# A routed-expert kernel on one Trainium2 core: gathers and row-number transfers held in program order, and another order of the composites

## The chip, the cores and the metric

The kernel runs on one core of one Trainium2 chip. The metric is the device time of one execution in microseconds (us). The core's engines are called as the profile calls them: PE is TensorE (PEld its weight loads), DVE VectorE, ACT ScalarE, POOL GpSimd, SP SyncE. SP only issues transfers here; POOL issues the indirect ones.

## What is computed

Two stages on an input `x` of 8 x 2880 x 192. First a causal 7-tap convolution per head, with softmax-normalised taps. Then each of the N = 23040 tokens is routed in two levels (the best of 4 groups, then the best of that group's 4 experts), and its one expert's two-layer network is applied:

```
x = attn_out.reshape(B * S, D)                    # 23040 x 192
g_idx = argmax(x @ w_group);  g_w = softmax(...)[g_idx]
for g in range(4):
    e_idx = argmax(x[g_idx == g] @ w_expert[g]);  e_w = softmax(...)[e_idx]
    for e in range(4):
        h  = maximum(xg[mask_e] @ w1[g, e], 0.0)  # 192 -> 1024
        ye = h @ w2[g, e]                         # 1024 -> 192
        out[tok_idx] = (g_w * e_w)[:, None] * ye
```

## The kernel before

**Units.** Convolution and routing run in units, mixed into the first half of the span. They write each token's row (196 numbers, its routing weight among them) to `xcd` in memory, and each token's row number into a table `idtab`, sorted by expert. When all tokens are routed, the table is closed: `close_table` writes 16 fills behind the experts' ends (L856, shown as `idtab<-seen`, on SP).

**Plan.** Expert work is a list of slots. The first 64 are full slots of 256 rows in three portions (one, two and one slot of each of the 16 experts); their row numbers are tiles `idp`. What each expert has left goes into 16 *composites*, whose row numbers are the tile `idpt`. A composite has one or two pieces, with row counts in `PIECES`: composites 0 and 1 are 320 + 320, 5 to 8 are 128 + 320, 9 to 11 are 384, 12 and 13 are 320, 14 and 15 are 256. `RANKS` is the order in which the composites run. Each full slot and each piece is a slot of the plan.

**One slot.** `gather` fetches its rows by indirect transfer on POOL (L674), 128 rows to a tile, into one of four buffers `xg`; a slot of 320 rows has a third tile of 64 rows, one of 384 a third of 128. The 64 full slots have no third tile. `turn` transposes the tiles on PE (L689, L690). `hidden` (L710; `hidden_wide`, L787, for over 256 rows) is the first layer, `back` (L728, L732; wide L805, L811) the second. `finish` scales on ACT (L822), adds the two halves on DVE (L829; a 64-row tile by L826 and L827), and stores through POOL (L830).

**Weights.** `weights` loads one expert's matrices on SP's queue by four transfers (L623, L624 and twice L626) into a ring of raw buffers; each is then split into a high and a low part by ACT and DVE (on DVE L639 for `al`, L643 for `bb`, L651 for `cw`).

**Opening the tail.** `open_tail` is a generator that is stepped at each opened slot: it closes the table, and then for each composite in the order of `RANKS` reads where its rows begin (L1046, SP) and transfers its row numbers (`tail_ids`, L1093 and, for a 64-row piece, L1095, `idpt<-idtab`, SP).

**Order.** A scheduler orders each engine's instructions; it may put an instruction ahead of others on its engine unless a dependence or an explicit hold binds it. Instructions then run in that order on each engine, each waiting for its own inputs and buffers.

**Rare block.** Tokens beyond the fixed plan are handled in a block under `tc.If` (L1190), which this input does not enter. It stands in front of the last slot of the plan; before it, all that is pending is finished.

Of the kernel before, what the change touches and what calls it, by code (L numbers as in the profile page):

```python
# [1 line left out]

# [12 lines left out]
U32 = mybir.dt.uint32  # L15
# [3 lines left out]
ET = mybir.EngineType  # L19
# [12 lines left out]
OOB_WHY = "the table's entries are clamped by construction"  # L32
# [3 lines left out]
def conv_moe_kernel(  # L36
# [10 lines left out]
    nc = tc.nc  # L47
# [9 lines left out]
    def pin(on, ins):  # L57

        return tc.keep_in_program_order(ins) if on and pinned[0] else ins
# [19 lines left out]
    PIECES = (  # L79
        [(320, 320)] * 2 + [(320, 256)] * 2 + [(256, 256)] + [(128, 320)] * 4 + [(384,)] * 3 + [(320,)] * 2 + [(256,)] * 2)  # L80
    CAPS = [sum(p) for p in PIECES]
    MOST, WMAX = CAPS[0], max(w for p in PIECES for w in p)
    NTAIL = len(PIECES)
    RANKS = [5, 2, 6, 3, 7, 4, 8, 0, 9, 14, 1, 10, 12, 11, 13, 15]
    assert NTAIL == E and sorted(RANKS) == list(range(E)) and sorted(CAPS, reverse=True) == CAPS
    CAP = -(-(N + MOST) // 1024) * 1024
    DUMMY = E * CAP
# [102 lines left out]
    xcd = dram.tile([N, XW], F32, name="xcd")  # L190
# [102 lines left out]
    for g in range(NSK):  # L293
        nc.sync.dma_start(
            out=skew[0:R, g * HG:(g + 1) * HG],
            in_=bass.AP(wvd.tensor, wvd.offset + VL - KS - (BT - 1) + g * HG * VL, [[1, R], [VL, HG], [1, VW]]),
# [15 lines left out]
    for h in range(H):  # L312
        nc.scalar.activation(
            out=band[0:R, h], in_=skew[0:R, h, BT - 1::-1], func=AF.Exp, bias=wm[0:R, h:h + 1],
# [10 lines left out]
    for k, (p0, r0, n) in enumerate(((0, 0, P), (0, P, D2), (D2, P, D2))):  # L325
# [10 lines left out]
        out=tri, in_=ones, pattern=[[1, P]], compare_op=ALU.is_gt, fill=0.0, base=0, channel_multiplier=-1,  # L336
# [10 lines left out]
    for nb in sorted({n for _, n in units}):  # L347
# [32 lines left out]
        out=sel[:, 0:E], in_=ident.rearrange("p (e l) -> p e l", e=E), axis=AX.X, op=ALU.add)  # L380
    nc.gpsimd.iota(io[:, 0:1], pattern=[[0, 1]], base=0, channel_multiplier=1)
    nc.vector.tensor_scalar(
        out=io[:, 1:2], in0=io[:, 0:1], scalar1=LE - 1, scalar2=None, op0=ALU.bitwise_and)
# [8 lines left out]
        out=eold[:, :, E:E + 1], in_=goff.unsqueeze(1).broadcast_to([P, NU + 1, 1]))  # L392
# [219 lines left out]
        finished(u)  # L612


    def weights(r1, r2, eng=None):
        eng = eng or {}
        raw = [wraw.tile([P, F], F32, name="raw") for _ in range(4)]
        ra, rb = raw[0], raw[1]
        HF = NF // 2
        rc = [r[:, 0:HF * D].rearrange("p (f d) -> p f d", d=D) for r in raw[2:]]  # L620
        npin[0] += 1
        hold = tc.keep_in_program_order if NPIN[0] < npin[0] <= NPIN[1] else lambda ins: ins
        hold(nc.sync.dma_start(out=ra, in_=w1f[bass.ds(r1, P), :]))  # L623
        hold(nc.sync.dma_start(out=rb[0:D2], in_=w1f[bass.ds(r1 + P, D2), :]))  # L624
        for k in range(2):
            hold(nc.sync.dma_start(  # L626
                out=rc[k], in_=w2f[bass.ds(r2 + k * HF * P, HF * P), :].rearrange("(f p) d -> p f d", p=P),
            ))
        W = {}

        def split(k):
            if k == 0:
                W["ah"] = ah = wsp.tile([P, F], F32R, name="ah")
                W["al"] = al = wsp.tile([P, F], F32R, name="al")
                if 8 in eng:
                    nc.gpsimd.tensor_copy(out=ah, in_=ra)
                else:
                    pin(PINA, nc.scalar.activation(out=ah, in_=ra, func=AF.Copy))  # L638
                eng.get(k, nc.vector).tensor_tensor(out=al, in0=ra, in1=ah.bitcast(F32), op=ALU.subtract)  # L639
            elif k == 1:  # L640
                W["bb"] = bb = wsp.tile([P, F], F32R, name="bb")
                pin(PINB, nc.scalar.activation(out=bb[0:D2], in_=rb[0:D2], func=AF.Copy))
                eng.get(k, nc.vector).tensor_tensor(  # L643
                    out=bb[D2:P], in0=rb[0:D2], in1=bb[0:D2].bitcast(F32), op=ALU.subtract)
            else:
                if k == 2:
                    W["cw"] = wsp.tile([P, NF, 2, D], F32R, name="cw")
                cw = W["cw"]
                fs = slice((k - 2) * HF, (k - 1) * HF)
                pin(PINW, nc.scalar.activation(out=cw[:, fs, 0, :], in_=rc[k - 2], func=AF.Copy))  # L650
                eng.get(k, nc.vector).tensor_tensor(  # L651
                    out=cw[:, fs, 1, :], in0=rc[k - 2], in1=cw[:, fs, 0, :].bitcast(F32), op=ALU.subtract,
                )

        W["todo"] = [lambda k=k: split(k) for k in range(4)]
        return W
# [9 lines left out]
    def split_rows(w):  # L666

        return [min(P, w - k) for k in range(0, w, P)]

    def gather(ids, known, w=SLOT):  # L670
        xs = xg[nslot[0] % NXG]
        nslot[0] += 1
        for t, n in enumerate(split_rows(w)):
            nc.gpsimd.indirect_dma_start(  # L674
                out=xs[0:n, t, :], out_offset=None, in_=xcd[0:known, :],
                in_offset=bass.IndirectOffsetOnAxis(ap=ids[t].bitcast(U32), axis=0),
                bounds_check=known - 1, oob_is_err=False,
            )
        return xs

    def turn(xs, w=SLOT):
# [156 lines left out]
    def close_table():  # L838
        ei = const.tile([1, E], I32, name="ei")
        nc.vector.tensor_copy(out=ei, in_=eold[0:1, counted[0], 0:E])  # L840
        yield

        NR = MOST // P
        seen = const.tile([P, NR], I32, name="seen")
        nc.sync.dma_start(
            out=seen, in_=TABV[0:NR, :].rearrange("r c -> (r c)").unsqueeze(0).broadcast_to([P, NR]))
        yield
        yield
        tc.keep_in_program_order(nc.vector.tensor_scalar(
            out=seen, in0=seen, scalar1=0, scalar2=BIG, op0=ALU.bitwise_and, op1=ALU.bitwise_or))  # L850
        yield
        _, ends = nc.values_load_multi_w_load_instructions(
            ei, engines=[ET.SP], min_val=0, max_val=DUMMY - MOST, skip_runtime_bounds_check_because=OOB_WHY,
        )
        for e in range(E):
            nc.sync.dma_start(  # L856
                out=idviews[1 + e % (len(idviews) - 1)][bass.ds(ends[e], MOST), :].rearrange("(p r) c -> p (r c)", p=P),
                in_=seen,
            )
            if e % 4 == 3:  # L860
                yield
# [171 lines left out]
    tab = [None]  # L1033
# [3 lines left out]
    idps = {}  # L1037
    late = []

    def open_tail():  # L1040
        yield from close_table()
        for tab[0] in table():
            yield
        idps["tail"] = const.tile([P, NTAIL, NID], I32, name="idpt")
        for j in RANKS:
            row = nc.values_load(  # L1046
                tab[0][0:1, j, 2:3], engines=[ET.SP], min_val=0, max_val=DUMMY,
                skip_runtime_bounds_check_because=OOB_WHY,
            )
            tail_ids(row, idps["tail"][:, j], PIECES[j])  # L1050
            yield

    def open_portion(pi):
# [35 lines left out]
    def tail_ids(row, idt, pieces=(SLOT,)):  # L1089
        n = sum(w // P for w in pieces)  # L1090
        m = sum(pieces) // XT - 2 * n
        rows = idtab[bass.ds(row, sum(pieces)), :]
        nc.sync.dma_start(out=idt[:, 0:n], in_=rows[0:n * P].rearrange("(p r) c -> p (r c)", r=n))  # L1093
        if m:
            nc.sync.dma_start(  # L1095
                out=idt[0:XT, n:n + m], in_=rows[n * P:n * P + m * XT].rearrange("(p r) c -> p (r c)", r=m))
# [8 lines left out]
    plan = [(pi, e, s) for pi, (_, spe) in enumerate(portions) for e in range(E) for s in range(spe)]  # L1105
    plan += [("tail", j, k) for j in RANKS for k in range(len(PIECES[j]))]
    weights_at = {}
# [44 lines left out]
    while routed[1] < portions[0][0]:  # L1152
        step()
        if k == 4:
            clear_table()
        for i in [i for i, kk in enumerate(KPRE) if kk == k]:
            e, q = divmod(i, 5)
            if q == 0 and e < 2:
                pre[e] = weights(e * D, e * F, {k: nc.gpsimd for k in PREG[e]})
            elif e < 2 and 4 * e + q <= KN:  # L1160
                split_one(pre[e])
        k += 1
# [83 lines left out]
    for i, (pi, e, s) in enumerate(plan):  # L1246
# [3 lines left out]
        W, ids = opened[i]  # L1250
        w = width(i)
        n = min(w, SLOT) // P
# [89 lines left out]
```

## Time and profile before

| | us |
|---|---|
| median of 3 runs | 1144.63 |
| lowest and highest | 1143.6, 1149.39 |
| the profiled execution | 1137.87 |
| span of the profiled execution | 1136.1 |
| mean granted clock of PE in it | 0.979 of full speed |

The profile is of one execution. A timeline row gives the start, the duration, the engine, the line and operation, out<-in, and, in brackets, how long the engine stood idle before it and what ended that. A q behind an engine's name (SPq, DVEq) is its sequencer, which issues transfers and runs branches. The granted clock of 1.00 is the higher of PE's two levels, 2.4 GHz, and 0.50 the lower, 1.2 GHz.

### The profile page before, as it was taken

To read this page: it belongs to the slowest core of one execution; us is meant where nothing else is said; L and a number is where in the kernel's file an instruction comes from. 1 tells how busy PE (TensorE), PEld (TensorE's weight loads), DVE (VectorE), ACT (ScalarE), POOL (GpSimd) and SP (SyncE) were. 2 spreads that over 40 slices of the span, in tenths; PEclk is the share of its full clock that TensorE was granted. 3 is DMA by queue.
4 is the path that set the end of the run, shared out by engine and by line. 5 is a ranking of instruction groups with operands and counts; after the bars stand their busy time and mean duration, and the time that the engine had idled before them with its cause. 6 is when DMAs were issued, how large, how long until landed. Compare 5 with 4: busy or idle time off the path is not lost. (4 is left out here: it accounts for less than half of the span.)

```text
span 1136.1 us, 23048 instructions
## 1 busy us (share of the span) xinstructions
PE 1087.7 (96%) x8170; PEld 1060.3 (93%) x8170; DVE 794.3 (70%) x1761; ACT 719.6 (63%) x1427; POOL 461.7 (41%) x420
## 2 busy tenths in 40 slices
PE   6799999999999999999999996999999999999995
PEld 5679899999999999999999996999999999999995
DVE  3747967887866666675678665888876766767772
ACT  4545576666775665656655664777776666666661
POOL 2003432234342534343435435555455454454531
PEclk9978999999999999999999998999999999999998
DMA  8879778879873564435354446777764444444420
GB/s 198 239 182 240 187 180 210 222 171 244 215 204 115 127 165 119 132 99 152 99 140 102 128 83 175 208 207 209 201 179 109 120 122 118 121 118 123 121 79 20
DMA packets 185203, 175.68 MB, mean 155 GB/s; under 512 B 47101, under 2 KB 166938, under 8 KB 185082
## 3 DMA queue, kind: packets, MB, share of 16 engines
q1 hardware_dynamic: 120108, 120.00, 39.2%
q0 software_dynamic: 18336, 36.08, 11.4%
q10 hardware_dynamic: 46638, 18.07, 7.4%
q8 instruction: 65, 1.06, 0.4%
q14 instruction: 56, 0.46, 0.1%
HBM read 138.23 MB, written 36.47 MB: 154 GB/s over the span
## 5 line engine op out<-in xcount | busy, mean ns | idle before, releaser
L728 PE MATMUL po<-cw,hh 128*128 128x384 f32 x1120 | 353.0, 372 | 0.4 <-ACT ys L822 0.4
L710 PE MATMUL ph<-xa,ah 128*128 128x256 f32 x1120 | 307.8, 296 | 4.4 <-DVEq L1190 2.4
L732 PE MATMUL po<-cw,hl 128*128 128x192 f32 x1120 | 281.2, 251 | 0.0
L715 ACT ACTIVATE hh<-ph 128x512 fp32r<-128x512 f32 x280 | 166.3, 595 | 162.7 <-PE ph L710 150.3
L674 POOL DMA_INDIRECT xg<-xcd,idp x128 | 143.1, 1118 | 306.6 <-ACT ys L822 275.6
L716 DVE SCALAR_TENSOR_TENSOR hl<-ph,hh 128x512 fp32r<-128x512 f32 x280 | 191.3, 686 | 92.9 <-ACT hh L715 89.7
L710 PE MATMUL ph<-xb,bb 128*128 128x256 f32 x1120 | 226.0, 283 | 0.0
L710 PEld LDWEIGHTS ph<-xa,ah 128*128 128x128 f32 x1120 | 212.3, 190 | 7.7 <-issue 2.7
L732 PEld LDWEIGHTS po<-cw,hl 128*128 128x128 f32 x1120 | 214.8, 192 | 1.9
L728 PEld LDWEIGHTS po<-cw,hh 128*128 128x128 f32 x1120 | 211.7, 189 | 2.9 <-ACT ys L822 0.6
L830 POOL DMA_INDIRECT out<-ys,idp x128 | 155.5, 1215 | 48.4 <-issue 30.1
L710 PEld LDWEIGHTS ph<-xb,bb 128*128 128x128 f32 x1120 | 173.2, 190 | 0.0
L710 PE MATMUL ph<-xa,al 128*128 128x256 f32 x560 | 158.3, 283 | 0.0
L822 ACT ACTIVATE ys<-po,xg 128x384 f32<-128x384 f32 x174 | 99.4, 581 | 77.2 <-PE po L732 41.5
L651 DVE TENSOR_TENSOR cw<-raw,cw 128x768 fp32r<-128x768 f32 x128 | 121.6, 952 | 19.3 <-ACT cw L650 17.4
L674 POOL DMA_INDIRECT xg<-xcd,idpt x61 | 69.2, 1135 | 136.7 <-ACT ys L822 95.2
L829 DVE TENSOR_TENSOR ys<-ys 128x192 f32<-128x192 f32 x177 | 62.6, 356 | 77.3 <-ACT ys L822 76.4
L650 ACT ACTIVATE cw<-raw 128x768 fp32r<-128x768 f32 x128 | 107.1, 842 | 4.2 <-DMA raw<-in_moe_w 4.1
L710 PEld LDWEIGHTS ph<-xa,al 128*128 128x128 f32 x560 | 107.5, 192 | 1.8
L639 DVE TENSOR_TENSOR al<-raw,ah 128x1024 fp32r<-128x1024 f32 x64 | 78.1, 1220 | 31.8 <-ACT ah L638 31.3
L830 POOL DMA_INDIRECT out<-ys,idpt x61 | 70.3, 1153 | 50.2 <-DVE ys L829 33.4
L638 ACT ACTIVATE ah<-raw 128x1024 fp32r<-128x1024 f32 x64 | 68.1, 1064 | 23.3 <-PE ph L710 10.1
(238 smaller groups left out, 1979.5 us busy)
## 6 DMA issues: line engine op xcount, KB each, us to landing
raw<-in_moe_w SPq DMA_DIRECT2D x128, 384.0 KB
raw<-in_moe_w SPq DMA_DIRECT2D x64, 512.0 KB
raw<-in_moe_w SPq DMA_DIRECT2D x64, 256.0 KB
xcd<-xc ACTq DMA_DIRECT2D x13, 742.5 KB
xin<-in_x SPq DMA_DIRECT2D x7, 1134.0 KB
xin<-in_x SPq DMA_DIRECT2D x6, 1039.5 KB
xcd<-xcb ACTq DMA_DIRECT2D x13, 360.0 KB
xg<-xcd,idp POOLq DMA_INDIRECT x128
```

Source lines behind the costliest of these rows:

```text
L638: pin(PINA, nc.scalar.activation(out=ah, in_=ra, func=AF.Copy))
L639: eng.get(k, nc.vector).tensor_tensor(out=al, in0=ra, in1=ah.bitcast(F32), op=ALU.subtract)
L650: pin(PINW, nc.scalar.activation(out=cw[:, fs, 0, :], in_=rc[k - 2], func=AF.Copy))
L651: eng.get(k, nc.vector).tensor_tensor(out=cw[:, fs, 1, :], in0=rc[k - 2], in1=cw[:, fs, 0, :].bitcast(F32), op=ALU.subtract,)
L674: nc.gpsimd.indirect_dma_start(out=xs[0:n, t, :], out_offset=None, in_=xcd[0:known, :], in_offset=bass.IndirectOffsetOnAxis(ap=ids[t].bitc ...
L710: nc.tensor.matmul(out=hp[:, j], lhsT=wgt[:, fs], rhs=xx, start=i == 0, stop=i == len(ops) - 1)
L715: nc.scalar.activation(out=hh, in_=hp, func=AF.Relu)
L716: nc.vector.scalar_tensor_tensor(out=hl, in0=hp, scalar=0.0, in1=hh.bitcast(F32), op0=ALU.max, op1=ALU.subtract,)
L728: nc.tensor.matmul(out=oo[t][:, 0:2 * D], lhsT=hh[:, j, ts], rhs=cw[:, f].rearrange("p a d -> p (a d)"), start=f == 0, stop=False,)
L732: nc.tensor.matmul(out=oo[t][:, 0:D], lhsT=hl[:, j, ts], rhs=cw[:, f, 0, :], start=False, stop=f == NF - 1,)
L822: nc.scalar.activation(out=y, in_=oo[t][0:n, 0:2 * D], func=AF.Copy, scale=g)
L830: nc.gpsimd.indirect_dma_start(out=outviews[nscat[0] % len(outviews)], out_offset=bass.IndirectOffsetOnAxis(ap=ids[t].bitcast(U32), axis=0 ...
```

## The change

Three things change. In `gather` a slot's third tile (t == 2) may be issued only after its second tile's gather. In `open_tail` the reading of a composite's start and its row-number transfers may be issued only after the weight transfer that was written last in the program (`loads[-1]`, the last L626 up to there). In `RANKS` composite 14 (256 rows) moves from the tenth place to the next to last, so that it, and not composite 13 (320 rows), stands in front of the rare block and of composite 15. The import adds a name; the lines of the changed kernel are 2 to 4 higher than those of before.

```
-    RANKS = [5, 2, 6, 3, 7, 4, 8, 0, 9, 14, 1, 10, 12, 11, 13, 15]
+    RANKS = [5, 2, 6, 3, 7, 4, 8, 0, 9, 1, 10, 12, 11, 13, 14, 15]
...
+    loads = []
+
     def weights(r1, r2, eng=None):
...
         for k in range(2):
-            hold(nc.sync.dma_start(
+            loads.append(nc.sync.dma_start(
                 out=rc[k], in_=w2f[bass.ds(r2 + k * HF * P, HF * P), :].rearrange("(f p) d -> p f d", p=P),
             ))
...
         for t, n in enumerate(split_rows(w)):
-            nc.gpsimd.indirect_dma_start(
-                out=xs[0:n, t, :], out_offset=None, in_=xcd[0:known, :],
-                in_offset=bass.IndirectOffsetOnAxis(ap=ids[t].bitcast(U32), axis=0),
-                bounds_check=known - 1, oob_is_err=False,
-            )
+            with tc.issue_after(ins.ins) if t == 2 else nullcontext():
+                ins = nc.gpsimd.indirect_dma_start(
+                    out=xs[0:n, t, :], out_offset=None, in_=xcd[0:known, :],
+                    in_offset=bass.IndirectOffsetOnAxis(ap=ids[t].bitcast(U32), axis=0),
+                    bounds_check=known - 1, oob_is_err=False,
+                )
...
         for j in RANKS:
-            row = nc.values_load(
-                tab[0][0:1, j, 2:3], engines=[ET.SP], min_val=0, max_val=DUMMY,
-                skip_runtime_bounds_check_because=OOB_WHY,
-            )
-            tail_ids(row, idps["tail"][:, j], PIECES[j])
+            with tc.issue_after(loads[-1].ins):
+                row = nc.values_load(
+                    tab[0][0:1, j, 2:3], engines=[ET.SP], min_val=0, max_val=DUMMY,
+                    skip_runtime_bounds_check_because=OOB_WHY,
+                )
+                tail_ids(row, idps["tail"][:, j], PIECES[j])
             yield
```

On SP, right behind the last fill write, two composites' row numbers stood ahead of the rest of a weight set (L626), and four more composites follow, before the next full set:

```order
L856 DMA idtab<-seen 128x5
L1046 TENSOR_LOAD tab
L1093 REGISTER_ALU
L1093 DMA idpt<-idtab 128x3
L1095 ISA
L1095 DMA idpt<-idtab 64x1
L1046 TENSOR_LOAD tab
L1093 REGISTER_ALU
L1093 DMA idpt<-idtab 128x4
L626 DMA raw<-in_moe_w 128x4x192
```

At the same place of the changed kernel the rest of that set and full sets (L625, L626 and twice L628) follow directly:

```order
L859 DMA idtab<-seen 128x5
L628 DMA raw<-in_moe_w 128x4x192 x2
L625 DMA raw<-in_moe_w 128x1024
L626 DMA raw<-in_moe_w 64x1024
L628 DMA raw<-in_moe_w 128x4x192 x2
```

Eight full sets stand there, and behind the eighth the first row numbers, one composite's after each set:

```order
L628 DMA raw<-in_moe_w 128x4x192 x2
L1050 TENSOR_LOAD tab
L1097 REGISTER_ALU
L1097 DMA idpt<-idtab 128x3
L1099 ISA
L1099 DMA idpt<-idtab 64x1
L625 DMA raw<-in_moe_w 128x1024
```

On POOL, two third tiles of 64 rows (their row numbers from `idpt`) stood among the gathers and stores of full slots (`xg_236` and the like are the four buffers):

```order
L830 DMA out<-ys,idp_3827 23040x192
L674 DMA xg_236<-xcd,idpt 64x196
L674 DMA xg_237<-xcd,idpt 64x196
L674 DMA xg_238<-xcd,idp_8896 128x196
L830 DMA out<-ys,idp_3827 23040x192
```

In the changed kernel they are gone from there and stand behind their own slots' second tiles, here in the composites:

```order
L677 DMA xg_236<-xcd,idpt 128x196
L833 DMA out<-ys,idp_8896 23040x192
L677 DMA xg_236<-xcd,idpt 64x196
L677 DMA xg_235<-xcd,idpt 128x196 x2
L677 DMA xg_237<-xcd,idpt 128x196
L833 DMA out<-ys,idp_8896 23040x192
L677 DMA xg_237<-xcd,idpt 128x196
L833 DMA out<-ys,idp_8896 23040x192
L677 DMA xg_237<-xcd,idpt 64x196
```

The two `xg_235` gathers in this piece are the second and third tile of a later 384-row composite; they stand ahead of the slot in `xg_237`, as they did before. What moved is the 64-row tile of `xg_237`, which is now the last of its three.

On DVE, ahead of the branch of the rare block (its flag is read by TENSOR_LOAD), the end of a 320-row composite's finish stood:

```order
L829 TENSOR_TENSOR ys<-ys 128x192 x2
L826 SCALAR_TENSOR_TENSOR ys<-ys,xg_238 64x192
L827 TENSOR_TENSOR ys<-ys 64x192
L1248 TENSOR_LOAD flagi
L1190 COMPARE_AND_BRANCH
```

Now one L832 (the L829 of before) stands there, of a 256-row composite, whose second one comes behind the block:

```order
L653 TENSOR_TENSOR cw<-raw,cw 128x4x192
L719 SCALAR_TENSOR_TENSOR hl<-ph,hh 128x512
L832 TENSOR_TENSOR ys<-ys 128x192
L1252 TENSOR_LOAD flagi
L1194 COMPARE_AND_BRANCH
```

The 64-row operations and one of the two additions are no longer ahead of the branch; the instructions ahead of them belong to the last hidden layer and the last weight split.

## Rows read from the trace of the kernel before

**Rows 1.** Busy time, share of the span and instructions of each engine

```profile
PE 1087.7 (96%) x8170; PEld 1060.3 (93%) x8170; DVE 794.3 (70%) x1761; ACT 719.6 (63%) x1427; POOL 461.7 (41%) x420
```

**Rows 2.** Timeline of PE (start, duration, operation, idle before) near 700 us

```profile
682.31 0.40 PE L710 MATMUL ph<-xb,bb 128*128 128x256 f32 x2
...
685.28 0.30 PE L710 MATMUL ph<-xa,ah 128*128 128x256 f32 x1
...
692.11 0.40 PE L710 MATMUL ph<-xb,bb 128*128 128x256 f32 x2
...
694.30 0.33 PE L689 MATMUL pm<-ident,xg 128*128 128x128 f32 x1 [1.79 <-DMA xg<-xcd,idp]
...
702.21 0.47 PE L689 MATMUL pm<-ident,xg 128*128 128x128 f32 x1 [7.46 <-DMA xg<-xcd,idp]
...
706.33 0.30 PE L710 MATMUL ph<-xa,ah 128*128 128x256 f32 x1
```

**Rows 3.** Timeline of POOL, the same stretch

```profile
686.14 0.99 POOL L674 DMA_INDIRECT xg<-xcd,idpt  x1 [14.83 <-DMA idpt<-idtab]
...
691.11 1.02 POOL L674 DMA_INDIRECT xg<-xcd,idp  x1 [0.30 <-issue]
...
694.48 1.04 POOL L674 DMA_INDIRECT xg<-xcd,idp  x1 [0.30 <-issue]
```

**Rows 4.** Timeline of SP's queue from the fill writes on

```profile
673.27 4.61 SPq L856 DMA_DIRECT2D idtab<-seen  x4
...
692.21 0.39 SPq L623 DMA_DIRECT2D raw<-in_moe_w  x1
...
757.77 0.34 SPq L623 DMA_DIRECT2D raw<-in_moe_w  x1
```

**Rows 5.** Timeline of DVE, splits of weights near 700 us

```profile
678.61 0.94 DVE L651 TENSOR_TENSOR cw<-raw,cw 128x768 fp32r<-128x768 f32 x1
...
699.18 1.22 DVE L643 TENSOR_TENSOR bb<-raw,bb 64x1024 fp32r<-64x1024 f32 x1 [0.77 <-ACT bb L642]
```

**Rows 6.** Timeline of PE around the branch and at the end

```profile
1112.24 0.54 PE L805 MATMUL pm<-cw,xc 128*128 128x384 f32 x2
...
1115.21 0.53 PE L710 MATMUL ph<-xa,ah 128*128 128x256 f32 x1 [2.44 <-DVEq L1190]
...
1118.53 0.34 PE L710 MATMUL ph<-xa,ah 128*128 128x256 f32 x1
...
1126.00 0.25 PE L732 MATMUL po<-cw,hl 128*128 128x192 f32 x1
```

**Rows 7.** Timeline of DVE at the same two places

```profile
1114.31 0.35 DVE L827 TENSOR_TENSOR ys<-ys 64x192 f32<-64x192 f32 x1
...
1126.38 0.36 DVE L829 TENSOR_TENSOR ys<-ys 128x192 f32<-128x192 f32 x1 [3.30 <-ACT ys L822]
```

**Rows 8.** Timeline of POOL in the composites

```profile
814.22 1.03 POOL L674 DMA_INDIRECT xg<-xcd,idpt  x1 [3.66 <-ACT ys L822]
...
837.72 1.99 POOL L674 DMA_INDIRECT xg<-xcd,idpt  x1 [4.93 <-DMA idpt<-idtab]
...
843.96 1.03 POOL L674 DMA_INDIRECT xg<-xcd,idpt  x1 [0.30 <-ACT ys L822]
...
847.13 1.01 POOL L674 DMA_INDIRECT xg<-xcd,idpt  x1 [0.30 <-ACT xc L790]
```

**Rows 9.** Timeline of PE in the composites

```profile
846.72 0.33 PE L689 MATMUL pm<-ident,xg 128*128 128x128 f32 x1 [0.25 <-DMA xg<-xcd,idpt]
...
847.74 0.27 PE L689 MATMUL pm<-ident,xg 128*128 128x128 f32 x1
```

**Rows 10.** Two stretches: us, busy time by engine, granted clock, DMA share, GB/s

```profile
694.00:695.00 1.00, 0.44 (x2) 0.17 (x2) 0.00 (x0) 0.00 (x0) 0.69 (x2) 1.00 1.02 385
...
1116.00:1117.00 1.00, 1.00 (x6) 1.00 (x6) 0.00 (x0) 0.00 (x0) 0.77 (x1) 0.50 0.41 121
```

**Rows 11.** Line 1190, PE's branches: durations in ns, first and last start

```profile
L1190 PEldq COMPARE_BRANCH  x2: 90/141/192, 1110.5 to 1113.1; - x2
```

More of the change, by code (lines that the diff above doesn't have):

```diff
@@ L1 @@
-from contextlib import ExitStack
+from contextlib import ExitStack, nullcontext
 import concourse.bass as bass
```

## The prediction, made before the changed kernel ran

> **What bounds the kernel now.** I read the busy-time view first. TensorE (PE) works for 96% of the span, and the next engine, VectorE (DVE), for 70% [rows 1]. So only two things can move the end: time in which PE does nothing, and time in which it runs at half clock. The slices of the page show one clear dent, near 700 us, and a small one at the end. The change touches both places and takes no matmul out, so I read those two, and then the composite phase, through which the held instructions now run.
>
> *The dent near 700 us.* In the PE timeline the reader is to compare two passages from a slot's last hidden-layer matmul to the next slot's first: 682.31 to 685.28, which is 2.97 us, and 692.11 to 706.33, which is 14.22 us [rows 2]. The second lost 11.25 us. Its two transpositions waited 1.79 and 7.46 us for gathered rows; the rest of the loss is time at a lowered clock, seen in the 0.47 us of the transposition at 702.21 where the one at 694.30 took 0.33 [rows 2].
>
> Who was late? The GpSimd (POOL) timeline shows that two row-number (idpt) gathers stood in front of the due ones: POOL waited 14.83 us for composite row numbers, until 686.14, waited again for the second, and only at 691.11 and 694.48 issued the two gathers that PE was waiting for [rows 3]. Both early ones are third tiles: buffers of four slots, whose third tile no portion slot uses, so nothing held them back.
>
> The weights were late too, and this must be said, because either alone would leave PE waiting. On SP's queue the fill writes end at 673.27 + 4.61 = 677.88; then, by the order, come the row-number transfers of six composites; and the next expert's weight load starts only at 692.21 [rows 4]. Its buffer had been free since about 678.61 + 0.94 = 679.55, the end of the DVE split that read it last [rows 5]. The last split of that weight set ended at 699.18 + 1.22 = 700.40 [rows 5], where PE's usual passage wanted it at 692.11 + 2.97 = 695.08. Gathers landed at 702.2, weights were ready at 700.4: two causes with nearly one end.
>
> *The dent at the end.* The last composite stands behind a branch (the rare block, L1190), and everything ahead of it is drained. PE's last matmul ends at 1112.24 + 0.54 = 1112.78 and the next starts at 1115.21, with DVE's branch as releaser; then PE runs at half clock until about 1118.53 [rows 6, 7]. What it waits for is the finish of a 320-row composite: two L829, then the 64-row piece L826 and L827, which ends at 1114.31 + 0.35 = 1114.66 [rows 7].
>
> **The change part by part.**
>
> *Third tile behind the second.* The two gathers leave the head of POOL's queue, and so do their waits. *Row numbers behind the weights.* By the order of the changed kernel SP now issues, after the fill writes, the rest of one weight set and then eight sets before the first row-number transfer. The two edits together return the 11.25 us: the gathers of 691.11 and 694.48 could have gone as soon as their buffer was read, and the weight set of 692.21 can go at about 679.6, which by the same 8.2 us from issue to last split (692.21 to 700.40) is ready at 687.8, well ahead of 695.08. Bounds of this term: 11.25 if both arrive, and 11.25 − (700.40 − 695.08) = 5.9 if the weights stay as late as they were. I take 11.25, as nothing else waits on that queue.
>
> What the wait costs elsewhere: the first row-number transfer now stands behind the weight set that was issued at 757.77 [rows 4], less the 11 us returned about 747. Its first reader is the gather at 814.22, then about 803 [rows 8]. That is 55 us of margin. From there one composite's numbers follow each weight set. I cost it at nothing; without that margin POOL would be held as before, 14.83 us at a time [rows 3].
>
> *New wait in the composites.* In before the third tile of a composite's second piece had often been gathered long ahead (the second of the two early gathers near 690 us is such a one). Now it stands in its place, and at one point that place is late. In POOL's new order, as in the old, the second and third tile of a later composite (two gathers, the first of which waited 4.93 us until 837.72) stand ahead of a 320-row piece whose second tile goes at 843.96 [rows 8]. PE wanted that second tile at 846.72 and waited 0.25 us for it [rows 9], so its gather took 846.72 − 843.96 = 2.76 us to land. The third tile was wanted at 847.74 [rows 9] and was there. Now it is issued behind the second tile's gather and the store after it, where 847.13 stands today [rows 8], and lands at about 847.13 + 2.76 = 849.9: PE waits 2.1 us, say 2.0. Bounds: 0, if the earlier phase moves by 11 us and the 4.93 us wait on row numbers goes with it; and 7.1, if it takes as long as the 694.48 gather did (702.21 − 694.48 = 7.7 us with the DMA share at 1.02 [rows 10]). I stay near the row beside it. The other moved third tiles have at least 3 us between landing and use.
>
> *A 256-row composite in front of the rare block.* Its finish has no 64-row piece, and by the order only the first of its two L829 stands ahead of DVE's branch. The last composite shows that timing: last matmul ends at 1126.00 + 0.25 = 1126.25, the first L829 at 1126.38 + 0.36 = 1126.74, so 0.49 us later [rows 7]. From DVE's last operation to PE's restart 1115.21 − 1114.66 = 0.55 us pass. The pause is then 0.49 + 0.55 = 1.04 instead of 2.43: 1.4 us. The half clock behind it, 1115.21 to 1118.53, is 3.32 us in which half, 1.66, is lost. A pause of 1.79 us at 692.5 was followed by full clock (694 to 695 at 1.00 [rows 10]), one of 2.43 by half (1116 to 1117 at 0.50 [rows 10]); so a pause of 1.04 should keep full clock, and 1.66 goes too. Bounds: 0 and 3.05. I take 3.05. Swapping the positions of composites moves no work: the same pieces run.
>
> *Sum.* 11.25 + 1.4 + 1.66 − 2.0 = 12.3 us. The profiled execution took 1137.87 us, its span 1136.1; from that 1125.6. The median of the runs shown is 1144.63, 6.8 above the profiled one; the change takes the same microseconds from both, so **1144.63 − 12.3 = 1132.3, say 1132**.
>
> **The rivals.**
>
> *A. The pause at the branch stays.* If PE's restart follows its own branch and not DVE, the 3.05 us stay: 1144.63 − 9.25 = 1135.4. Against it: PE's two branch instructions there took at most 0.192 us and the last started by 1113.1 [rows 11], while PE went on at 1115.21, after DVE's. For it: the row cannot tell a stall that ends with DVE's branch from one that would have ended there anyway. The Trainium skill speaks for this rival, in "Runtime: NRT & Kernel Launch", section "Instruction fetch mechanics": a taken branch whose target lies outside the two pages held makes the engine fetch the page before it goes on. By that rule the time would be this rival's; the trace, with 0.192 us for the longer of PE's branches, does not bear it out.
>
> *B. Weights still late.* If the held loads do not move forward (the fill writes end only at 677.88 and the DMA engines are full), PE waits for the weights to 700.40 as before: 5.3 us stay, 1137.6. Against it: no transfer of SP's stands between 677.88 and the weights any more.
>
> *C. Held third tiles cost what they gave.* The piece at 847 waits 7.1 instead of 2.0, and the later composite's early pair, which the change leaves where it was (it holds only the third tile, not the second behind the first), repeats its wait in front of another piece for about as long as the 1.79 us: 1144.63 − 14.3 + 7.1 + 1.8 = 1139.2. The change then does only half of what it says.
>
> *D. Slower: row numbers arrive late.* If row-number transfers slip behind weight sets that themselves wait for buffers, POOL stands at its queue's head for numbers that SP has not issued, and each such event costs what the one at 700 us cost, 11.25. It decides from a slip of 55 us on, and two events make the change slower: 1144.63 − 12.3 + 2 × 11.25 = 1154.8. For it: in before waits of that kind stood in the composites too, 4.93 us at 837.72 [rows 8]. Against it: from 692.21 to 757.77 [rows 4] SP issued eight weight sets, one each 9.4 us, so 55 us are nearly six sets.
>
> **How the numbers follow.** The forecast 0.62, A 0.12, B 0.09, C 0.10, D 0.07. The range of 8 in 10 takes the forecast with the bounds of its terms, A and B: above, 1139, where C stands; below, 1144.63 − 14.3 = 1130.3 with no new wait, and, since the profiled execution ran 6.8 under the median, on down to about its own figure, 1125.6: 1125 to 1139. Half a per cent, about what a measurement of this kernel can tell, is 5.7 us: faster below 1138.9, slower above 1150.4. Faster holds the forecast, A and B, 0.83; the same is C, 0.10; slower is D, 0.07.
>
> **What would show it.** Right: no stretch near 690 us in which PE waits for a gather, and the passage there again near 3.0 us; SP's weight loads straight behind the fill writes; row numbers not before about 745 us; a wait of about 2 us for an xg third tile near 837; a pause of about 1.0 us at the branch with full clock after it. Wrong: PE waiting for splits near 684 (B), the pause at the branch above 2 us though DVE is done (A), POOL waiting on row numbers with PE idle behind it (C, D).

## The result, and the profile after

| | before | after |
|---|---|---|
| median of 20 runs each, us | 1148.62 | 1136.79 |
| lowest and highest | 1142.98, 1159.32 | 1131.27, 1145.63 |
| profiled execution, us | 1137.87 | 1133.7 |

The ratio is 0.9894, with a 95% interval of 0.9866 to 0.9921: faster by 1.06%, 12.2 us of 1148.62. The forecast gain was 12.3 us, the forecast time 1132, the range 1125 to 1139. The time before, over more runs, is 4 us higher than the three runs shown had it, and 1148.62 − 12.3 is 1136.3.

The two profiled executions are only 4.2 us apart. Before the first changed instruction runs, the execution after was already 4.4 us late: the start of the 34th expert's split, `ah<-raw` on ACT, stood at 668.10 in the first profile of before and stands at 672.50 here. So the stretches are compared by their own length, between starts of such splits (one in each weight set; all 64 are in every trace). The rows of the profile after:

```profile
672.50 1.06 ACT L640 ACTIVATE ah<-raw 128x1024 fp32r<-128x1024 f32 x1 [0.35 <-issue]
...
712.37 1.06 ACT L640 ACTIVATE ah<-raw 128x1024 fp32r<-128x1024 f32 x1
...
819.69 1.06 ACT L640 ACTIVATE ah<-raw 128x1024 fp32r<-128x1024 f32 x1
...
876.08 1.06 ACT L640 ACTIVATE ah<-raw 128x1024 fp32r<-128x1024 f32 x1 [0.35 <-PE ph L713]
```

Here the stretch around 700 us, from the 34th split to the 38th, lasts 712.37 − 672.50 = 39.87 us, and the composites' first stretch, from the 49th to the 52nd, 876.08 − 819.69 = 56.39 us. In the first profile of before these were 51.15 (668.10 to 719.25) and 50.11 (826.69 to 876.80; such differences of rounded starts can be off by 0.01). So 11.28 us were returned at 700 us, and 6.28 us lost again 130 us later.

**Around 690 us.** What answers to [rows 2] in PE's timeline, one slot's last hidden matmul and the next slot's first, twice:

```profile
686.71 0.40 PE L713 MATMUL ph<-xb,bb 128*128 128x256 f32 x2
...
689.68 0.30 PE L713 MATMUL ph<-xa,ah 128*128 128x256 f32 x1
...
696.51 0.40 PE L713 MATMUL ph<-xb,bb 128*128 128x256 f32 x2
...
699.49 0.30 PE L713 MATMUL ph<-xa,ah 128*128 128x256 f32 x1
```

689.68 − 686.71 = 2.97 and 699.49 − 696.51 = 2.98: no wait and no lowered clock is left (the granted clock from 686 to 700 us is 1.00). On POOL, what answers to [rows 3]: the due gathers go out in front, with nothing ahead of them that waits for row numbers:

```profile
684.25 1.19 POOL L677 DMA_INDIRECT xg<-xcd,idp  x1 [0.30 <-issue]
...
690.16 1.04 POOL L677 DMA_INDIRECT xg<-xcd,idp  x1 [3.02 <-ACT ys L825]
```

On SP's queue, what answers to [rows 4]: the fill writes (16 in one row, to 680.71), then the weights, and the first row-number transfer only at 756.14:

```profile
666.75 13.96 SPq L859 DMA_DIRECT2D idtab<-seen  x16
...
680.82 0.94 SPq L628 DMA_DIRECT2D raw<-in_moe_w  x2
...
683.09 0.34 SPq L625 DMA_DIRECT2D raw<-in_moe_w  x1
...
756.14 0.35 SPq L1097 DMA_DIRECT2D idpt<-idtab  x1
```

**Around 840 us.** The stretch that grew. POOL, PE and ACT, and the clock behind it:

```profile
830.09 1.03 POOL L677 DMA_INDIRECT xg<-xcd,idpt  x1 [5.63 <-DMA idpt<-idtab]
...
835.64 1.03 POOL L677 DMA_INDIRECT xg<-xcd,idpt  x1 [0.30 <-issue]
...
838.31 0.97 POOL L677 DMA_INDIRECT xg<-xcd,idpt  x1 [0.30 <-issue]
```

```profile
839.43 0.27 PE L693 MATMUL pm<-ident,xg 128*64 128x128 f32 x1
...
840.50 0.27 PE L692 MATMUL pm<-ident,xg 128*128 128x128 f32 x1 [0.80 <-issue]
...
843.97 0.60 PE L790 MATMUL ph<-xa,ah 128*128 128x320 f32 x1 [3.20 <-DVE xc L796]
...
845.65 0.42 PE L692 MATMUL pm<-ident,xg 128*128 128x128 f32 x1
```

```profile
836.13 0.60 ACT L760 ACTIVATE hh<-pm 128x512 fp32r<-128x512 f32 x1 [0.86 <-PE po L735]
...
840.58 1.05 ACT L825 ACTIVATE ys<-po,xg 128x384 f32<-128x384 f32 x2 [3.85 <-DMA xg<-xcd,idpt]
...
842.26 0.76 ACT L793 ACTIVATE xc<-ph 128x320 fp32r<-128x320 f32 x2
```

A row by stretch gives its length, the busy time of PE, PEld, DVE, ACT and POOL with their instructions, the granted clock, the DMA share and GB/s:

```profile
834.00:838.00 4.00, 4.00 (x30) 3.99 (x29) 0.69 (x1) 1.20 (x2) 3.09 (x3) 1.00 0.92 269
842.00:844.00 2.00, 0.03 (x1) 0.06 (x1) 1.63 (x5) 2.00 (x5) 1.69 (x2) 0.50 0.20 50
844.00:848.00 4.00, 4.00 (x16) 3.87 (x17) 3.04 (x10) 2.17 (x6) 2.30 (x3) 0.50 0.69 208
```

POOL stood 5.63 us at the later composite's early gather, waiting for row numbers, and then issued everything that had queued behind it in one string (830.09 to 838.31 holds the early pair, the next slot's three tiles and two stores). PE waited 0.80 us for the second tile, which went out at 835.64 and was transposed at 840.50, then 3.20 us for an operation on DVE (L796) that itself waited for ACT; ACT stood 3.85 us at a slot's finish (L825) and went on at 840.58, which the profile puts down to the landing of a gather (more on this in "What stays open"). The granted clock is 0.50 from 842 to 848 us, so that PE, at work again from 843.97, ran at half speed. The third tile, at 845.65, was not waited for.

**At the branch.** PE's last matmul in front, the first two behind, and DVE's last operation in front, answering to [rows 6, 7]:

```profile
1110.75 0.25 PE L735 MATMUL po<-cw,hl 128*128 128x192 f32 x1
...
1111.99 0.35 PE L713 MATMUL ph<-xa,ah 128*128 128x256 f32 x1 [0.99 <-DVEq L1194]
...
1112.19 0.28 PE L713 MATMUL ph<-xa,al 128*128 128x256 f32 x1
```

```profile
1111.08 0.36 DVE L832 TENSOR_TENSOR ys<-ys 128x192 f32<-128x192 f32 x1 [2.15 <-ACT ys L825]
```

From 1110.75 + 0.25 = 1111.00 to 1111.99 is 0.99 us of pause where it was 2.43, and the first matmul takes 0.35 us where it took 0.53 [rows 6]. The granted clock from 1112 to 1116 us is 1.00.

### The profile page after: what moved, and what is told of

Read it like the earlier page. It is cut to its first block, busy times and chain, and to the rows that moved or that the text cites. A ratio compares the mean times of both kernels' runs of the same rounds, so it can differ in the third digit from the quotient of the medians.

```text
span 1132.0 us, 23042 instructions
## 1 busy us (share of the span) xinstructions
PE 1088.6 (96%) x8170; PEld 1060.3 (94%) x8170; DVE 794.5 (70%) x1761; ACT 719.9 (64%) x1427; POOL 464.6 (41%) x420
## 3 DMA queue, kind: packets, MB, share of 16 engines
q8 instruction: 65, 1.06, 0.4%
## 5 line engine op out<-in xcount | busy, mean ns | idle before, releaser
L825 ACT ACTIVATE ys<-po,xg 128x384 f32<-128x384 f32 x174 | 99.2, 582 | 74.9 <-PE po L735 37.2
L832 DVE TENSOR_TENSOR ys<-ys 128x192 f32<-128x192 f32 x177 | 62.7, 356 | 77.0 <-ACT ys L825 70.0
L790 PE MATMUL ph<-xa,ah 128*128 128x320 f32 (+1 forms) x240 | 76.6, 326 | 5.1 <-DVE xc L796 4.5
```

Of the source, the lines that this page charges most:

```text
L790: nc.tensor.matmul(out=hp[:, 0:w], lhsT=wgt[:, fs], rhs=xx, start=i == 0, stop=i == len(ops) - 1)
L825: nc.scalar.activation(out=y, in_=oo[t][0:n, 0:2 * D], func=AF.Copy, scale=g)
```

## The experiments

All times below are device times beside runs of the kernel before on the same chip; the ratio is to those. Beside each ratio I use the two stretches defined above, *the 700 stretch* (34th to 38th split) and *the 840 stretch* (49th to 52nd). Their undisturbed lengths, as the quietest runs below show them, are 39.9 and 49.8 us.

**Third tiles held, row numbers free.** Of the change only the `issue_after` in `gather`, with the old order of the composites:

```
+            with tc.issue_after(ins.ins) if t == 2 else nullcontext():
...
-            with tc.issue_after(loads[-1].ins):
+            with nullcontext():
```

> The kernel before with the third tiles held behind the second ones alone; the row numbers stay where they were. Theory (two late causes at 700 us, gathers to 702.2 and weights to 700.4): the gathers come in time, but row-number transfers still stand ahead of the weights, so PE's passage there shrinks from 14.2 us to about 8.3 (2.97 + 5.3), waiting for splits and not for gathers. Gain there 5.9 us, less the new wait in the composites near 840 us (6 us in the profile of the changed kernel): 0 to 4 us in all, a ratio of 0.997 to 1.000. Rival (the gathers alone were the cause): passage near 3 us, gain 5 to 9 us.

Ratio 0.9989 (0.9963 to 1.0014). The 700 stretch lasts 44.69 us: 4.8 over the quiet length, where 5.3 was expected and 11.3 stood in before. What PE waits for there is no gather. SP's row-number transfers stand ahead of the weights as before (the first at 692.35, the next full set at 702.22), and ACT waits for that set:

```profile
707.18 1.06 ACT L640 ACTIVATE ah<-raw 128x1024 fp32r<-128x1024 f32 x1 [6.02 <-DMA raw<-in_moe_w]
```

```profile
692.35 0.27 SPq L1097 DMA_DIRECT2D idpt<-idtab  x1
...
702.22 0.38 SPq L625 DMA_DIRECT2D raw<-in_moe_w  x1
```

```profile
711.52 0.39 PE L713 MATMUL ph<-xa,ah 128*128 128x256 f32 x1 [3.20 <-DVE hl L719]
```

ACT's hidden operations stand behind its split, which waited 6.02 us for weights, and PE waits 3.20 us for their result. So the second of the two causes is shown alone. The 840 stretch lasts 55.86 us, and takes back what the first one gave.

**Row numbers held, third tiles free**, again with the old order of the composites.

```
-            with tc.issue_after(ins.ins) if t == 2 else nullcontext():
+            with tc.issue_after(ins.ins) if False else nullcontext():
```

> The kernel before with the row-number transfers held behind the weights alone; third tiles free. By its order the scheduler then puts the two early third tiles far later on POOL, close to where their row numbers arrive. Theory (both waits at 700 us come from where the row numbers stand): passage near 3.0 us, 11.25 us gained; and as third tiles may be fetched early, no wait for them in the composites: gain about 11, ratio 0.990. Rival (third tiles, if not held, hold POOL again): POOL waits 10 us or more for row numbers near 760 us, PE waits behind it, gain under 5.

Ratio 0.9949 (0.9919 to 0.998). The 700 stretch is 39.87 us: all that before loses there is gained with the row numbers' hold alone. The early third tiles have moved to about 767 us, and the first of them waits there:

```profile
766.93 1.23 POOL L677 DMA_INDIRECT xg<-xcd,idpt  x1 [6.76 <-DMA idpt<-idtab]
```

Between the stretches (38th to 49th split) this run takes 108.77 us where nearly all others take 107.3 to 107.5: 1.4 us lost behind these waits, less than the rival said. The 840 stretch is 53.73, so 3.9 us are lost there although the third tiles are free; that I had not expected.

**The order of the composites alone**, on the kernel before (only the line of `RANKS`).

> The kernel before with the order of the composites alone changed (a 256-row one in front of the rare block). Theory: the pause of PE at the branch is 1.0 us instead of 2.4 and full clock follows: 3.1 us gained, ratio 0.997; the passage at 700 us stays at 14 us. Rival (the last composite's own branch sets the pause): pause still 2.4, nothing gained.

Ratio 0.9989 (0.9961 to 1.0016): the 3.1 us lie inside the interval, so the time alone decides nothing. The profile does:

```profile
1133.00 0.36 PE L710 MATMUL ph<-xa,ah 128*128 128x256 f32 x1 [0.99 <-DVEq L1190]
```

The pause is 0.99 us, and the first matmul behind it takes 0.36 us; in the second profile of before, below, it is 2.44 and 0.55. But the part of the span that the order can change did not shrink by 3.1 us: from the 59th split to the end it takes 121.2 us here (from 1031.94 in a span of 1153.1) and 122.5 in both profiles of before (from 1013.62 in 1136.1, from 1024.83 in 1147.3). Two waits of PE that before does not have, or has shorter, stand in it (1.20 us at 1052.04, before 0.70; 0.46 at 1137.25, before none).

**Both holds, old order of composites.** The changed kernel with the old line of `RANKS`.

> The changed kernel with the old order of the composites (both holds, a 320-row composite in front of the rare block). Theory: the 11.25 us at 700 us are gained, the pause at the branch is 2.4 us again. Near 840 us PE loses what the held third tile and the later composite's early pair cost: 2 us by the prediction, 6 by the profile of the changed kernel; if the 6 us stand here again they belong to the order of instructions, if not they were an accident of one execution. Gain 5 to 9 us, ratio 0.992 to 0.996.

Ratio 0.9948 (0.9919 to 0.9977), 6 us. The 700 stretch is 39.87, the 840 stretch 55.85: the loss stands again. Set beside the run with the row numbers held alone (0.9949, the same order of composites), this says what the third tiles' hold adds once the row numbers are held: nothing that these times show. By the profiles it gains 1.4 us between the stretches and loses 2.1 at 840 us.

**The kernel before and the changed one once more.** Was the loss at 840 us new, or had the first profile of before only escaped it?

> The kernel before once more, for a second profile of it. In its first profile PE lost 0.25 us near 840 us, where four variants and the changed kernel lost 5 to 6. Theory A (the loss near 840 belongs to the held third tile): the kernel before shows under 1 us there again. Theory B (the loss is one of every order that sends the gathers of three slots out together behind a wait for row numbers, and the first profile escaped it): it shows 4 to 6 us there.

> The changed kernel once more, for a second profile of it. If the loss near 840 us (6.2 us in its first profile) belongs to its order, it stands again with 4 to 6 us; if it was an accident, it is gone. The passage at 690 us near 3.0 us and the pause at the branch of 1.0 us with full clock behind it should repeat.

Ratios 0.9993 (0.9958 to 1.0028) and 0.9933 (0.9901 to 0.9965). The second profile of before, PE near 700 and 840 us and at the branch, POOL's wait for row numbers, and ACT's splits:

```profile
703.82 0.33 PE L689 MATMUL pm<-ident,xg 128*128 128x128 f32 x1 [0.31 <-DMA xg<-xcd,idp]
...
710.02 0.47 PE L689 MATMUL pm<-ident,xg 128*128 128x128 f32 x1 [5.77 <-DMA xg<-xcd,idp]
...
855.27 0.33 PE L689 MATMUL pm<-ident,xg 128*128 128x128 f32 x1 [0.86 <-issue]
...
861.08 0.38 PE L787 MATMUL ph<-xa,ah 128*128 128x320 f32 x1 [2.52 <-ACT xa L692]
...
1126.45 0.55 PE L710 MATMUL ph<-xa,ah 128*128 128x256 f32 x1 [2.44 <-DVEq L1190]
```

```profile
695.43 0.98 POOL L674 DMA_INDIRECT xg<-xcd,idpt  x1 [12.89 <-DMA idpt<-idtab]
```

```profile
679.34 1.06 ACT L638 ACTIVATE ah<-raw 128x1024 fp32r<-128x1024 f32 x1 [0.59 <-PE ph L710]
...
726.97 1.06 ACT L638 ACTIVATE ah<-raw 128x1024 fp32r<-128x1024 f32 x1
...
834.42 1.06 ACT L638 ACTIVATE ah<-raw 128x1024 fp32r<-128x1024 f32 x1
...
888.14 1.06 ACT L638 ACTIVATE ah<-raw 128x1024 fp32r<-128x1024 f32 x1 [0.35 <-PE ph L710]
```

The 700 stretch is 47.63 us here, so that PE lost 7.8 us there and not 11.3; POOL's wait for row numbers is 12.89 us instead of 14.83, and PE's first wait for gathered rows 0.31 instead of 1.79. And the 840 stretch is 53.72: before loses 3.9 us there too, which speaks against Theory A and is a little less than Theory B said. The changed kernel's second profile has 39.63 and 54.48.

**Every tile held; two composites' row numbers in a step.** Two ways to take POOL's wait in front of the 840 stretch away. The first extends the hold to the second tile, so that the later composite's pair no longer stands in front:

```
-            with tc.issue_after(ins.ins) if t == 2 else nullcontext():
+            with tc.issue_after(ins.ins) if t else nullcontext():
```

> The changed kernel with every tile of a slot held behind the one before it, so that the later 384-row composite's second and third tile no longer stand ahead of the slot that PE needs next. Theory: POOL no longer waits about 5 us for that composite's row numbers there, the slot's three tiles go out early, PE's loss near 840 us falls under 1 us; 2 us gained by the prediction's price, up to 6 by the profile of the changed kernel. Rival (the loss comes from the weight loads that use the DMA engines at that time, not from POOL's wait): loss unchanged, 4 to 6 us.

The second brings the row numbers earlier:

```
                 tail_ids(row, idps["tail"][:, j], PIECES[j])
-            yield
+            if RANKS.index(j) % 2:
+                yield
```

> The changed kernel with the row numbers of two composites, not one, issued in each step, so that all are there earlier. Theory: no gather of the composites waits for row numbers (POOL's waits of 5 us there go), the gathers spread out, PE's loss near 840 us falls under 1 us: 2 to 6 us gained over the changed kernel. Rival: the two more transfers in each step, or the weights behind them, cost as much; no gain.

Ratios, from four runs each, 0.9844 (0.9778 to 0.991) and 0.9867 (0.979 to 0.9943). The 840 stretch is 49.84 and 49.79: the loss is gone in both, while the weight loads stay. With every tile held, the later composites lose 1.8 us instead (52nd to 59th split in 138.59 us, 136.8 in the first profile of before).

> The changed kernel with both mends: every tile held behind the one before it, and two composites' row numbers in each step. Either alone took PE's loss near 840 us away. Theory: they mend the same thing, so together they give no more than one: 0 to 2 us against either alone, about 16 us (11 at 700, 3 at the branch, the rest in the composites) under the kernel before, ratio 0.985 to 0.988. Rival: the two mend different waits and add: another 4 us.

> Row numbers held behind the weights and two composites' in each step, third tiles free, the new order of composites. It asks whether the hold on third tiles is needed. Theory: not at 700 us (with the row numbers behind the weights the free third tiles go to about 760 us), but there two of them wait for row numbers at the head of POOL's queue, 3 to 7 us, and PE loses 1 to 2 us some 25 us later as in the run with row numbers alone; near 840 no loss. 1 to 2 us slower than with the hold. Rival: as fast as with it.

> The changed kernel with two composites' row numbers in each step, once more with more rounds, beside the changed kernel on the same chip: 4 to 6 us under it (the loss near 840 us), ratio to the kernel before 0.985 to 0.988, and no loss near 840 us in the profile.

> The changed kernel a third time, on the same chip as the mended ones: near 840 us again 4 to 6 us lost; ratio to the kernel before 0.989 to 0.993.

These four ran on one chip. Both mends: 0.9871 (0.9829 to 0.9912); two in a step, again: 0.9864 (0.9816 to 0.9911), median 1129.14 us; the changed kernel: 0.9906 (0.9871 to 0.994), median 1136.95. Within these intervals the mends do not add. The 840 stretch is 49.82 in both mended ones and 56.72 in the changed kernel. In the run with two in a step POOL issues the same slot's gathers with pauses that ACT's finish sets, none that row numbers set:

```profile
827.14 1.03 POOL L677 DMA_INDIRECT xg<-xcd,idpt  x1 [2.13 <-ACT ys L825]
...
830.36 1.18 POOL L677 DMA_INDIRECT xg<-xcd,idpt  x1 [0.30 <-issue]
...
833.56 0.97 POOL L677 DMA_INDIRECT xg<-xcd,idpt  x1 [0.31 <-issue]
```

Two in a step with free third tiles: 0.9909 (0.9883 to 0.9935). There two early third tiles stand together and wait 6.88 us for row numbers; the string of gathers and stores behind them ends as it does at 840, with PE idle in pieces:

```profile
766.21 1.11 POOL L677 DMA_INDIRECT xg<-xcd,idpt  x1 [6.88 <-DMA idpt<-idtab]
```

```profile
777.99 0.34 PE L731 MATMUL po<-cw,hh 128*128 128x384 f32 x1 [0.55 <-issue]
...
779.41 0.34 PE L731 MATMUL po<-cw,hh 128*128 128x384 f32 x1 [0.71 <-issue]
```

Between the 38th and 49th split it takes 112.22 us, 4.9 over the others, where I expected 1 to 2; its 840 stretch, 48.87 us, gives 1 us of it back. It is the clearest sight of what the third tiles' hold is good for: beside it the run with the hold had a median 7.8 us lower (1129.14 against 1136.91).

The stretches of all profiles together, in us (over the quiet length in brackets):

| profile | third tiles | row numbers | 700 stretch | 840 stretch |
|---|---|---|---|---|
| before, first | free | free | 51.14 (11.3) | 50.12 (0.3) |
| before, second | free | free | 47.63 (7.8) | 53.72 (3.9) |
| order of composites alone | free | free | 48.99 (9.1) | 55.24 (5.4) |
| third tiles alone | held | free | 44.69 (4.8) | 55.86 (6.1) |
| row numbers alone | free | held | 39.87 | 53.73 (3.9) |
| both, old order | held | held | 39.87 | 55.85 (6.0) |
| changed kernel, three | held | held | 39.87, 39.63, 39.67 | 56.38 (6.6), 54.48 (4.7), 56.72 (6.9) |
| every tile held | all held | held | 39.86 | 49.84 |
| two in a step, two | held | held | 39.87, 39.87 | 49.79, 49.82 |
| both mends | all held | held | 40.34 | 49.82 |
| two in a step, third tiles free | free | held | 39.87 | 48.87 |

## Why the prediction was right, and where it was only near

The time came out inside the range, and the forecast gain of 12.3 us is what the runs first gave (12.2). Two later sets of runs gave 0.9933 and 0.9906, 7.7 and 10.8 us, so that some 10 us is the better figure and the agreement to 0.1 us is luck. The steps one by one:

**The dent at 700 us: mechanism right, size from one profile.** Two causes with nearly one end, as the sum had it: with the gathers mended alone, 4.8 us stayed (5.3 worked out), and with both 11.28 were returned in the first pair of profiles (11.25 worked out). But this term is not a constant of the kernel. Three profiles with both third tiles and row numbers free lost 11.3, 7.8 and 9.1 us, 9.4 in the mean, and I read it from the worst of them. What I said of either cause alone was half wrong: the row numbers' hold alone takes both away, since the scheduler then lets the early third tiles go later. So it wasn't the two edits together that returned the dent; the hold on the row numbers did it. The margin of 55 us before the first reader is about what stands there: issue at 756.14, first use at 807.32, 51 us.

**The new wait near 840 us: the place right, tile, size and cover wrong.** The term was 2.0 us for a third tile. The changed kernel loses 6.6, 4.7 and 6.9 us there, the two other runs with held third tiles and POOL's wait 6.1 and 6.0; those with free third tiles 0.3, 3.9, 5.4 and 3.9. The means, 6.1 and 3.4, are 2.7 apart, but with a spread from 0.3 to 5.4 among four, that this difference belongs to the held third tiles isn't shown, and its nearness to the price is no support for it. I had taken the place for undisturbed, because the first profile of before was: 0.25 us of PE's time in [rows 9], 0.3 in the stretch. And it isn't the third tile that is late. In the first profile of the changed kernel it is the second one, by 0.80 us; then PE stands 3.20 us behind ACT and DVE; the rest, 6.28 − 0.80 − 3.20 = 2.28 us, falls to PE's work at half clock behind that. The bound of 7.1 held all. The landing that I took from the nearest row, 2.76 us, was 840.50 − 835.64 = 4.86 us in that crowd. The Trainium skill gives a fit for such a transfer in "DMA: Bandwidth & Descriptors", section "Anatomy of one DMA — SWDGE (gpsimd) path", of 2.0 us plus the bytes over 436e3 per us, by an estimate 2.2 us for these 128 rows of 784 bytes; the trace doesn't agree where many transfers are out at once (4.86 us from the start of issue to use here, with a DMA share of 0.92 from 834 to 838 us).

**The branch: the pause right, the half clock behind it no constant.** The pause is 0.99 us in all three profiles of the changed kernel and with the order of the composites alone (1.04 worked out), and full clock follows: 1.44 us of pause are gained. The 1.66 us of half clock were read from one profile as the price of a 2.43 us pause, and they aren't that. Five profiles have the old order of composites and a pause of 2.44 us. In both of before the clock is 0.50 right behind it; with both holds it falls about 0.9 us after the restart (0.50 from 1119 to 1121 us); in the other two, with one hold each, it stays at 1.00. Here the row numbers' hold alone (the clock is the third figure from the end of the second row):

```profile
1119.03 0.35 PE L713 MATMUL ph<-xa,ah 128*128 128x256 f32 x1 [2.44 <-DVEq L1194]
```

```profile
1119.00:1121.00 2.00, 1.97 (x16) 2.00 (x17) 0.00 (x0) 0.46 (x1) 1.28 (x2) 1.00 0.22 66
```

From the 59th split to the end, before took 122.5 us in both profiles and the changed kernel 119.0, 120.5 and 120.4: 2.5 us in the mean, not 3.1. Rival A is out: the restart followed DVE, whose L832 ends at 1111.44, by 0.55 us as before. The Trainium skill's rule on taken branches, in "Runtime: NRT & Kernel Launch", section "Instruction fetch mechanics", says that a taken branch whose target lies outside the pages held stalls for a fetch, and gives no length. The trace doesn't bear out that it set the long pause; what a fetch may cost PE here lies inside the 0.99 us that are left.

**The rivals.** B is out: weights went from 680.82 on, and nothing waited for them at 690. Its ground that the DMA engines were full was wrong as well: in the profile of before their share is 0.02 in the 5 us behind the fill writes, the column before the last:

```profile
678.00:683.00 5.00, 5.00 (x42) 5.00 (x41) 4.94 (x7) 3.42 (x6) 0.00 (x0) 1.00 0.02 1
```

C was right in its mechanism, as the early pair of the later composite kept its place and held POOL 5.63 us; the runs with every tile held and with two composites in a step show that without this wait, by either end, the 840 stretch loses nothing. It was wrong in that before pays part of it as well. D did not come at 700 us; a small case of it, 6.8 us of POOL's wait, came when third tiles were free and row numbers held.

So the sum by what the runs showed: 9.4 + 2.5 − 2.7 = 9.2 us. Taken whole, from the 34th split to the end, both profiles of before last 468.0 us and those of the changed kernel 459.5, 459.2 and 460.7: 8.2 us. The timed runs lie around that, at 12.2, 7.7 and 10.8. That the forecast of 12.3 met the first of them is owed to the dent's size in the one profile and to the half clock, both too large, against a first measurement that was the largest of three.

**What stays open.** Why ACT and PE stood in the 840 stretch is shown by its condition only: of nine profiles in which POOL had waited there for row numbers and then issued gathers and stores in one string, eight lost 3.9 to 6.9 us, and the first one of before 0.3; of the five without that wait none lost anything there. The profile puts ACT's 3.85 us down to the landing of a gather, though that finish doesn't read the tile that landed then. The signals in the trace (the semaphore updates by which one engine releases another) point elsewhere. ACT's wait for the gathers' signals is recorded at 836.13 and lasts 0.04 us; what that finish still needed was a signal of PE. PE has eight matmuls that give one between 836.33 and 839.10, but none of their signals is recorded before 840.56; then nine come within 0.4 us, and ACT goes on at 840.58. Such a gap, with a burst behind it, also stands in the runs with the third tiles alone (847.36 to 853.42) and with both holds in the old order (839.98 to 844.34). In all eight profiles with the loss ACT's longest wait there ends 0.02 to 0.03 us behind a signal of PE. So ACT waited for PE and not for a gather. Whether PE's signals were late or PE itself was, and what held them while POOL's string was out, is not shown (some records can be missing from a trace), and no run tried it.

## What to carry to other kernels

An instruction that waits at the head of an in-order queue charges everything behind it (here POOL waited 14.83 and 12.89 us). So the transfers that feed a prefetch are held behind loads with an earlier reader; that alone returned the dent. The prefetch itself, which a scheduler may hoist, is then held behind the work that is due first: that hold made no difference in time with one composite's row numbers in a step (0.9949 and 0.9948), and 4.9 us between the stretches with two. Then look for the next such wait on the same queue: here the changed kernel still had one, and issuing two composites' row numbers in a step took its 840 stretch from 54.5 and 56.7 us to 49.8. In medians on one chip that is 1129.14 against 1136.95 us, and 1133.84 against 1140.94 on another; the intervals of the ratios overlap both times, so the times alone don't settle the size. A loss read from a single profile is the size of that execution; if the sum hangs on it, read it from two. The same holds for a clock that falls behind a pause: of five profiles with one and the same pause, three showed it.

## What was not expected

The spread between executions: before the first changed instruction, the same program's 34th split started between 668.1 and 683.4 us over all the profiles here, and the first profiled execution of before, 1137.87 us, was faster than each of the 20 timed ones (1142.98 at the lowest). The dent at 700 us differed by 3.5 us between two executions of one kernel, and the loss near 840 us by 3.6; in the sum over both stretches the two executions of before differ by 0.1 us (11.6 and 11.7).
